# Output tiles summed in SBUF by VectorE, or copied by ScalarE and added to DRAM by transfers

## The chip, the cores and the metric

The kernel runs on one core of one Trainium2 chip. The core has five engines that run side by side, each with its own queue of instructions in a fixed order: TensorE (PE, matmuls), VectorE (DVE), ScalarE (ACT), GpSimd (POOL) and SyncE (SP, which here only issues transfers). They meet at semaphores: an instruction waits until another engine, or a transfer, has counted a semaphore up to a value. Transfers between DRAM (HBM) and on-chip memory (SBUF) can be issued from SP, ACT and POOL; sixteen transfer engines carry them out. PE writes its results to PSUM, which transfers and POOL don't read, so ACT or DVE must take them out.

The metric is the time on the device from start to end, in microseconds (us).

## The reference

For 2048 positions of 576 numbers, two branches over the same normalised input are added to the input:

```
xn  = layernorm(x)                                   # eps 1e-5, no weights
A   = attention(xn @ wqkv) @ wo                      # 32 heads of 18; each position sees
                                                     # itself and 7 earlier ones, 2 apart
B   = relu(xn @ w1) @ w2                             # 576 -> 4608 -> 576
out = x + A + B                                      # fp32
```

## The kernel before

Rows of x are taken so that row 16p + 2i + phase lies in partition p of tile i of a phase. There are two phases (even and odd rows), each with 8 tiles (i = 0..7) of 128 rows; because attention steps by 2, a phase never needs the other's rows. A tile is 128 partitions x 576 columns, 288 KB.

To come near fp32 accuracy, PE's operands are split into a high and a low part (`two`, `transpose_split`, `h_out`: ACT makes the high part, DVE subtracts to get the low part, for some early weights POOL does), and every product is a sum of matmuls of these parts.

The backbone is the feed-forward branch. Its hidden dimension is cut into 36 blocks of 128 columns; three blocks make a chunk, so a phase has 12 chunks. For each chunk the kernel walks over four pairs of tiles (tb = 0..3), and for each pair over the chunk's three blocks (f = 0..2). That gives 2 x 12 x 4 x 3 = 288 slots, in one list. In slot n:

- `run_splits` splits weights that are due and issues further weight loads on SP, through five staging buffers `st`;
- `h_mm` for slot n + 2: fourteen matmuls into a PSUM tile `ph` (two of these), then ACT's relu `hhi` (line 563) and DVE's `hlo` (line 566);
- whatever the plan has put into this slot (`todo`);
- `o_mm` for slot n: twelve matmuls from `hhi`, `hlo` and w2 into two PSUM tiles `po`, one for each tile of the pair. They collect over the three blocks; after the third, `o_out` adds them into the tiles of x in SBUF (line 620, DVE);
- what the plan has put behind (`todo_late`);
- `run_bg`: pieces of attention on DVE, in a queue `bg`. A piece is put in when the planner's own sum of DVE's costs (`t["dve"]`, raised by `dve(n)`) is no more than a margin ahead of its sum for PE (`t["pe"]`). So what is taken from DVE's sum moves attention pieces to earlier slots.

x tiles live in a pool `xp` of 11 buffers. A tile is loaded (`load_x`, line 245 on SP, or ACT for tile 1), gets its mean and variance (`stats`, lines 257 to 264, the reciprocal root on POOL), is normalised into `xn` (`norm`, line 276/277 on ACT or 279 on DVE), is transposed on PE (`make_xt`, lines 293/294) and split into `xT`. After that it stays as the accumulator of its output rows. In the other phase's preparation four tiles are transposed by DVE and DRAM instead of PE.

Four attention units per phase (8 heads each) have 8 steps of `qkv_tile` (q, k, v of one tile through PSUM tiles `pm`, copied out by ACT), then a queue of DVE pieces. One piece, the mask (line 434), is on POOL; the maximum on DVE (line 440) follows it. When the units are done, the wo product of each tile follows: `wo_a` transposes by 32 x 32 blocks on DVE and stores them to DRAM (`turned`), `wo_f` loads them back, `wo_s` splits, and `wo_b` multiplies by wo into two `pm` tiles, which DVE adds into the tile of x in two column ranges (`CUT`: 256 and 320; line 529). `done` counts for each tile the two last additions, the wo one and that of the last chunk; at the second SP stores the tile (line 537).

The head, before slot 4, is written out by hand: loads, statistics, transposes and the first three blocks in an order that follows the arrival of the data. `HEAD` lists what of it is left for slots 4 to 6, among it the statistics, normalisation and transposes of tiles 6 and 7. The end is by hand too: in the last slot each tile's additions and stores are in two column ranges (lines 626, 628).

Of the kernel before, what the change touches and what calls it, by code (L numbers as in the profile page):

```python
# [10 lines left out]
F32 = mybir.dt.float32  # L11
# [6 lines left out]
P = 128  # L18
NPH = 2
# [20 lines left out]
FIRST = 4  # L40

HEAD = (
    (4, 0, 'stats', 6, False, True),
    (4, 1, 'norm', 6, True),
    (4, 1, 'stats', 7),
# [10 lines left out]
def tile_body(ctx: ExitStack, tc: tile.TileContext, x, wqkv, wo, w1, w2, out):  # L56
# [15 lines left out]
    ctx.enter_context(tc.manual_schedule())  # L72
    pool = lambda name, bufs, **k: ctx.enter_context(tc.tile_pool(name=name, bufs=bufs, **k))
    consts = pool("consts", 1)
    xp = pool("xp", 11)
    xtp = pool("xtp", NTB)
    qop = pool("qop", 1)
    kp = pool("kp", 1)
# [33 lines left out]
    def mm(o, l, r, start, stop, n):  # L112
        nc.tensor.matmul(o, l, r, start=start, stop=stop)  # L113
        t["pe"] += n / 2400.0 + 0.002

    def dve(n):
        t["dve"] += (n + 130) / 960.0
# [403 lines left out]
    def wo_b(ph, i):  # L521
        d, w = OT.pop((ph, i)), WO[ph]
        po = [ps_m.tile([P, c.stop - c.start], F32, name="pm") for c in CUT]
        for j, (a, b) in enumerate(TERMS):
            for h, c in enumerate(CUT):
                mm(po[h], d[a], w[b][:, c], j == 0, j == len(TERMS) - 1, D2)
        for h, c in enumerate(CUT):
            acc = X[ph, i][:, c]
            nc.vector.tensor_tensor(acc, po[h], acc, op=ALU.add)  # L529
            dve(D2)  # L530

    left = {(ph, i): 2 for ph in range(NPH) for i in range(NI)}

    def done(ph, i):
        left[ph, i] -= 1
        if left[ph, i] == 0:
            nc.sync.dma_start(o_v[ph, i], X[ph, i])


    slots = [(ph, c, tb, f) for ph in range(NPH) for c in range(NCH) for tb in range(NTB) for f in range(C)]  # L540
# [38 lines left out]
    def half(po, h):  # L579
        if isinstance(po, list):  # L580
            return po[h]
        return po[:, 1, 0 : D - 256] if h else po[:, 0, 256:512]
# [28 lines left out]
    def o_out(n, which=range(2)):  # L611
        ph, c, tb, f = slots[n]
        if f < C - 1:
            return
        for k in which:
            i = 2 * tb + k
            acc = X[ph, i]
            if n < len(slots) - 1:
                whole = PO[k].rearrange("p b c -> p (b c)")[:, 256 : 256 + D]
                nc.vector.tensor_tensor(acc, whole, acc, op=ALU.add)  # L620
                dve(D)
                if c == NCH - 1:
                    done(ph, i)
                continue
            for h, c in reversed(list(enumerate(CUT))):
                nc.vector.tensor_tensor(acc[:, c], half(PO[k], h), acc[:, c], op=ALU.add)  # L626
                if k:
                    (nc.scalar if h else nc.sync).dma_start(o_v[ph, i][:, c], acc[:, c])
            if k == 0:
                done(ph, i)  # L630


    todo = {}
# [1 line left out]
    def at(n, f, *a):  # L635
        todo.setdefault(n, []).append((f, a))
# [7 lines left out]
    for ph in range(NPH):  # L644
        b = ph * SPP
        for c in range(NCH):
            for f in range(C):
                s = b + c * SPC + f
                first = ph == c == 0
                plan.append((HEADW[f] if first else s - 5, w1_task, ((ph, c, f), c * C + f)))  # L650
                plan.append((HEADW[3 + f] if first else s - 3, w2_task, ((ph, c, f), c * C + f)))
        for u in range(NU):
            s = b + UNIT0 + u * UNIT_STEP
            plan.append((s - 5, wq_tasks, ((ph, u), u)))
            for i in range(NI):
                at(s + i, qkv_tile, ph, u, i)
            late(s + NI + 1, attention, ph, u)
        s = b + UNIT0 + NU * UNIT_STEP + WO_AT
        plan.append((s - 8, wo_tasks, (ph,)))
        for i in range(NI):  # L660
            z = s + WO_STEPS[i]
            late(z, wo_a, ph, i)
            at(z + 1, wo_f, ph, i)
            late(z + 3, wo_s, ph, i)
            at(z + 4, wo_b, ph, i)
            at(z + 4, done, ph, i)
        if ph + 1 < NPH:
            e = b + SPP - SPC
            for i in range(NI):
                if i >= len(XT_STEPS):  # L670
                    z = e + 3 + 2 * i
                    at(z - 6, load_x, ph + 1, i)
                    late(z - 2, stats, ph + 1, i)
                    late(z - 1, norm, ph + 1, i)
                    at(z + 1, make_xt, ph + 1, i)
                    continue
                load, first, second, send, back, parts = (e + k for k in XT_STEPS[i])
                at(load, load_x, ph + 1, i)
                late(first, stats, ph + 1, i, False, True)
                late(second, norm_turned, ph + 1, i)  # L680
                late(send, xt_a, ph + 1, i)
                at(back, xt_f, ph + 1, i)
                at(parts, xt_s, ph + 1, i)
# [27 lines left out]
    h_terms(0, both)  # L711
    run_splits(-8)
    stage_more(4)
    for i in range(4, NI):
        load_x(0, i)
    stats(0, 2)
    for z in x0[2:], x1[2:]:
        for f in z:
# [46 lines left out]
    make_xt(0, 5, bank=ps_h)  # L765
    o_mm(3, which=(1,))
    for z, k, op, *a in HEAD:
        (late if k else at)(z, {"stats": stats, "norm": norm, "xt": make_xt}[op], 0, *a)
    M = (3.0, 1.5, 3.0)
    AT_WO = range(UNIT0 + NU * UNIT_STEP + WO_AT, UNIT0 + NU * UNIT_STEP + WO_AT + 12)  # L770
    for n in range(FIRST, len(slots)):
# [42 lines left out]
```

## Time and profile before

| | |
|---|---|
| median of 3 runs | 1167.42 us (1166.56 to 1168.52) |
| span of the profiled execution, first to last instruction | 1163.8 us |
| PE busy | 1155.9 us |
| DVE busy | 822.9 us |
| ACT busy | 308.1 us |
| POOL busy | 44.9 us |
| moved by transfers | 88.66 MB, a mean of 76 GB/s |

For the profiled execution the profile gives the span; the runs' times hold what lies around it as well.

How the profile's rows are read: L12 is line 12 of the kernel. A group's row has line, engine, operation, output<-inputs, their shapes and how many there are, then busy time in us and the mean of one in ns, then the idle time of the engine just before them with what ended most of it. A row of waits says which engine and line waited for which, with the total in us, the number of times and the longest. A row of a timeline begins with start and duration in us; x4 means that four instructions are merged. A row of windows has the stretch, its length, each engine's busy time and (x instructions), the granted clock of PE, the busy share of the transfer engines and GB/s. PEld is PE's loading of weights, which runs beside its matmuls; SPq and ACTq are transfers being issued. The chain is the work that ended last, followed back from the last instruction.

### The profile page before, as it was taken

What the parts mean: (1) busy time and instruction counts of PE and PEld (TensorE: products, weight loads), DVE (VectorE), ACT (ScalarE), POOL (GpSimd) and SP (SyncE); (2) the same over time, 40 slices, a digit from 0 to 9 for tenths busy, and PEclk for the clock granted to TensorE, in tenths of its full rate; (3) what the DMA queues carried; (4) which work ended last, traced back from release to release, by engine and by line L of the source; (5) the groups of instructions that cost most, each with busy time, mean ns of one, the idle gap of its engine ahead of it and who ended that gap; (6) DMA issues with size and microseconds to landing.
All of it is one profiled execution on the core that took longest, in us unless ns stands there. A gap on an engine that the chain in (4) does not pass through costs nothing.

```text
span 1163.8 us, 21695 instructions
## 1 busy us (share of the span) xinstructions
PE 1155.9 (99%) x8916; PEld 1147.9 (99%) x8916; DVE 822.9 (71%) x1300; ACT 308.1 (26%) x747; POOL 44.9 (4%) x60
## 2 busy tenths in 40 slices
PE   8999999999999999999999999999999999999998
PEld 8999999999999999999999999999999999999998
DVE  7427885887687688876683288768858877887843
ACT  4422222131231212322433123222222312222210
POOL 2200100010000000000010001000100000000000
PEclk9999999999999999999999999999999999999999
DMA  6303221140321211365752113021312303113541
GB/s 184 98 23 85 65 55 53 40 112 1 94 76 34 82 32 52 96 151 116 175 170 66 46 53 94 22 77 36 92 34 62 110 1 101 44 32 97 123 100 63
DMA packets 149732, 88.66 MB, mean 76 GB/s; under 512 B 58512, under 2 KB 133264, under 8 KB 149632
## 3 DMA queue, kind: packets, MB, share of 16 engines
q1 hardware_dynamic: 146656, 78.54, 25.1%
q10 hardware_dynamic: 2976, 8.72, 2.6%
q8 instruction: 70, 1.15, 0.4%
q14 instruction: 30, 0.25, 0.1%
HBM read 67.90 MB, written 11.14 MB: 68 GB/s over the span
## 4 chain that ended last, share of the span: by engine, by line
PE 99%; issue 0%; DVE 0%; DMA 0%; POOL 0%; ACT 0%; SPq 0%; DVEq 0%; POOLq 0%
PE ph L113 39%; PE po L113 38%; PE pm L113 20%; PE pm L293 0%; DMA x<-in_x 0%; DVE x L626 0%; POOL rstd L264 0%; PE pm L294 0%; PE po L293 0%; ACT xT L298 0%; DVE xn L279 0%; DVE bst L257 0%; SPq L243 0%; DVEq L810 0%; PE ph L294 0%
## 5 line engine op out<-in xcount | busy, mean ns | idle before, releaser
L113 PE MATMUL ph<-xT,w1t 128*128 128x256 f32 x4018 | 505.0, 277 | 0.7 <-ACT xT L298 0.7
L113 PEld LDWEIGHTS ph<-xT,w1t 128*128 128x128 f32 x4018 | 486.8, 188 | 1.3 <-ACT xT L298 1.0
L113 PE MATMUL po<-w2t,hhi 128*128 128x256 f32 x2292 | 393.0, 293 | 0.0
L113 PEld LDWEIGHTS po<-w2t,hhi 128*128 128x128 f32 x2292 | 335.4, 188 | 1.1
L563 ACT ACTIVATE hhi<-ph 128x256 fp32r<-128x256 f32 x287 | 110.0, 384 | 582.2 <-PE ph L113 568.9
L113 PE MATMUL po<-w2t,hlo 128*128 128x256 f32 x1146 | 242.4, 292 | 0.0
L566 DVE SCALAR_TENSOR_TENSOR hlo<-ph,hhi 128x256 fp32r<-128x256 f32 x287 | 121.0, 422 | 164.5 <-ACT hhi L563 164.0
L113 PEld LDWEIGHTS po<-w2t,hlo 128*128 128x128 f32 x1146 | 188.9, 187 | 0.0
L620 DVE TENSOR_TENSOR x<-po,x 128x576 f32<-128x576 f32 x190 | 143.1, 757 | 60.1 <-PE po L113 57.2
L113 PE MATMUL pm<-wq,xT 128*128 128x432 f32 x896 | 185.5, 358 | 0.0
L113 PEld LDWEIGHTS pm<-wq,xT 128*128 128x128 f32 x896 | 163.8, 188 | 5.6
L428 DVE TENSOR_TENSOR pr<-qo,k 128x1152 f32<-128x1152 f32 x64 | 86.1, 1349 | 0.0
L431 DVE TENSOR_REDUCE lg<-pr 128x64 f32<-128x1152 f32 x64 | 85.1, 1343 | 0.0
L458 DVE TENSOR_TENSOR pr<-lg,v 128x1152 f32<-128x1152 f32 x64 | 84.7, 1350 | 0.0
L152 DVE TENSOR_TENSOR w2t<-st,w2t 128x576 fp32r<-128x576 f32 x72 | 55.8, 775 | 32.4 <-ACT w2t L148 32.3
L152 DVE TENSOR_TENSOR w1t<-st,w1t 128x640 fp32r<-128x640 f32 x70 | 58.9, 841 | 20.6 <-ACT w1t L148 20.5
L465 DVE TENSOR_TENSOR pr<-pr 128x288 f32<-128x288 f32 (+1 forms) x128 | 70.6, 601 | 0.0
L148 ACT ACTIVATE w2t<-st 128x576 fp32r<-128x576 f32 x72 | 49.3, 684 | 44.9 <-PE po L113 32.5
L397 ACT ACTIVATE k<-pm 128x144 f32<-128x144 f32 x64 | 18.7, 292 | 146.3 <-PE pm L113 146.3
L148 ACT ACTIVATE w1t<-st 128x640 fp32r<-128x640 f32 x71 | 52.1, 734 | 11.7 <-DMA k<-k 6.0
L434 POOL TENSOR_SCALAR_AFFINE_SELECT lg<-lg 1x512 f32<-1x512 f32 x8 | 9.9, 1234 | 809.6 <-DVE lg L431 809.6
L529 DVE TENSOR_TENSOR x<-pm,x 128x256 f32<-128x256 f32 (+1 forms) x32 | 13.1, 453 | 30.2 <-PE pm L113 30.2
(85 smaller groups left out, 470.0 us busy)
## 6 DMA issues: line engine op xcount, KB each, us to landing
st<-in_w SPq DMA_DIRECT2D x72, 288.0 KB, 3.1
st<-in_w SPq DMA_DIRECT2D x72, 256.0 KB, 3.2
st<-in_wqkv SPq DMA_DIRECT2D x32, 216.0 KB, 3.0
turned<-tr SPq DMA_DIRECT2D x64, 80.0 KB, 3.0
xn<-turned SPq DMA_DIRECT2D x16, 320.0 KB, 3.2
st<-in_w SPq DMA_DIRECT2D x142, 32.0 KB, 2.9
out<-x SPq DMA_DIRECT2D x15, 288.0 KB, 2.1
x<-in_x SPq DMA_DIRECT2D x14, 288.0 KB, 4.3
```

What stands on the lines that cost most here:

```text
L113: nc.tensor.matmul(o, l, r, start=start, stop=stop)
L148: nc.scalar.activation(hi, src, AF.Copy)
L152: nc.vector.tensor_tensor(lo, src, f32(hi), op=ALU.subtract)
L397: nc.scalar.activation(k[:, W - 1 + i, :], pq[:, 1, :], AF.Copy)
L428: nc.vector.tensor_tensor(pr[i], q, window(k, i), op=ALU.mult)
L431: nc.vector.tensor_reduce(lg[:, i], pr.pop(i).rearrange(heads, d=Dh), axis=AX.X, op=ALU.add)
L458: nc.vector.tensor_tensor(pr[i].rearrange(heads, d=Dh), e, window(v, i).rearrange(heads, d=Dh), op=ALU.mult)
L465: nc.vector.tensor_tensor(o, z[:, 0:n], z[:, n : 2 * n], op=ALU.add)
L529: nc.vector.tensor_tensor(acc, po[h], acc, op=ALU.add)
L563: nc.scalar.activation(hi, pt, AF.Relu)
L566: nc.vector.scalar_tensor_tensor(lo, pt, 0.0, f32(hi), op0=ALU.max, op1=ALU.subtract)
L620: nc.vector.tensor_tensor(acc, whole, acc, op=ALU.add)
```

## The change

The output in DRAM becomes the accumulator. Early in the head SP issues one transfer that copies all of x into the output, 4.72 MB. From then on each finished tile, of `o_out` (190 whole ones, and two in halves at the end) and of `wo_b` (16), is copied from PSUM by ACT into one of four new buffers `ev`, and POOL issues a transfer that adds the buffer to the tile's rows of the output. x tiles aren't accumulators any more, so they are free after normalisation: `xp` shrinks from 11 to 6 buffers, and tiles 6 and 7 of the first phase are loaded in slot 4 in place of the head. `done` and its stores go. DVE's part of the planner's costs no longer has the additions.

In the built program PE's instructions are the same, in the same order. SP's copy stands where the load of tile 6 stood. POOL has 210 adding transfers in its queue. The first two stand between the reciprocal roots of tiles 4 and 5 and the subtractions for the first attention weights (wq); the first waits for the copy. Each transfer waits for ACT's copy and the transfer eight before it, some also for an earlier one of the same tile; a copy on ACT waits for the transfer four before it.

```diff
 HEAD = (
+    (4, 0, 'load', 6),
+    (4, 0, 'load', 7),
     (4, 0, 'stats', 6, False, True),
...
-    xp = pool("xp", 11)
+    xp = pool("xp", 6)
+    evp = pool("evp", 4)
...
         for j, (a, b) in enumerate(TERMS):
             for h, c in enumerate(CUT):
                 mm(po[h], d[a], w[b][:, c], j == 0, j == len(TERMS) - 1, D2)
+        ev = evp.tile([P, D], F32, name="ev")
         for h, c in enumerate(CUT):
-            acc = X[ph, i][:, c]
-            nc.vector.tensor_tensor(acc, po[h], acc, op=ALU.add)
-            dve(D2)
-
-    left = {(ph, i): 2 for ph in range(NPH) for i in range(NI)}
-
-    def done(ph, i):
-        left[ph, i] -= 1
-        if left[ph, i] == 0:
-            nc.sync.dma_start(o_v[ph, i], X[ph, i])
+            nc.scalar.activation(ev[:, c], po[h], AF.Copy)
+        add_out(ph, i, ev)
+
+    def add_out(ph, i, ev):
+        nc.gpsimd.dma_start(o_v[ph, i], ev, accum_op=ALU.add)
...
         for k in which:
             i = 2 * tb + k
-            acc = X[ph, i]
+            ev = evp.tile([P, D], F32, name="ev")
             if n < len(slots) - 1:
                 whole = PO[k].rearrange("p b c -> p (b c)")[:, 256 : 256 + D]
-                nc.vector.tensor_tensor(acc, whole, acc, op=ALU.add)
-                dve(D)
-                if c == NCH - 1:
-                    done(ph, i)
+                nc.scalar.activation(ev, whole, AF.Copy)
+                add_out(ph, i, ev)
                 continue
             for h, c in reversed(list(enumerate(CUT))):
-                nc.vector.tensor_tensor(acc[:, c], half(PO[k], h), acc[:, c], op=ALU.add)
-                if k:
-                    (nc.scalar if h else nc.sync).dma_start(o_v[ph, i][:, c], acc[:, c])
-            if k == 0:
-                done(ph, i)
+                nc.scalar.activation(ev[:, c], half(PO[k], h), AF.Copy)
+                nc.gpsimd.dma_start(o_v[ph, i][:, c], ev[:, c], accum_op=ALU.add)
...
-            at(z + 4, done, ph, i)
...
     stage_more(4)
-    for i in range(4, NI):
+    for i in range(4, 6):
         load_x(0, i)
+    nc.sync.dma_start(out.rearrange("(p r) d -> p (r d)", p=P), x.rearrange("(p r) d -> p (r d)", p=P))
     stats(0, 2)
...
     for z, k, op, *a in HEAD:
-        (late if k else at)(z, {"stats": stats, "norm": norm, "xt": make_xt}[op], 0, *a)
+        (late if k else at)(z, {"load": load_x, "stats": stats, "norm": norm, "xt": make_xt}[op], 0, *a)
```

## The prediction

> **What bounds the kernel now.** I read the page first: busy times, slices, the chain, the groups.
>
> ```profile
> span 1163.8 us, 21695 instructions
> PE 1155.9 (99%) x8916; PEld 1147.9 (99%) x8916; DVE 822.9 (71%) x1300; ACT 308.1 (26%) x747; POOL 44.9 (4%) x60
> PE 99%; issue 0%; DVE 0%; DMA 0%; POOL 0%; ACT 0%; SPq 0%; DVEq 0%; POOLq 0%
> L563 ACT ACTIVATE hhi<-ph 128x256 fp32r<-128x256 f32 x287 | 110.0, 384 | 582.2 <-PE ph L113 568.9
> L620 DVE TENSOR_TENSOR x<-po,x 128x576 f32<-128x576 f32 x190 | 143.1, 757 | 60.1 <-PE po L113 57.2
> L113 PE MATMUL ph<-xT,w1t 128*128 128x256 f32 x4018 | 505.0, 277 | 0.7 <-ACT xT L298 0.7
> ```
>
> PE is the chain: 1155.9 of 1163.8 us. ACT spends 569 us waiting for PE, and the 190 adds of L620 wait for PE too (57.2 us). Next I asked what PE itself waited for, over the whole span.
>
> ```profile
> PE po L293 <- DVE xn L279: 1.8, 1, 1.8
> PE po L104 <- POOL mhalf L99: 1.4, 1, 1.4
> PE ph L113 <- ACT xT L298: 0.7, 1, 0.7
> PE pm L293 <- ACT xn L277: 0.3, 1, 0.3
> ```
>
> Four waits, 4.2 us together, once each, before the first transposes and the first ph; PE never waits for an add. So the 143 us of adds in L620, and the 32 smaller ones of the wo steps, that the change takes off DVE buy nothing: PE's matmuls are the same in number and order, and its idle time is 7.9 us in all. What the change can do is put a wait into PE's queue, at the head, in the loop or at the end.
>
> **The head: a transfer ahead of two loads.** In a timeline of the first 40 us, SP's queue and the work on tile 6 of x:
>
> ```profile
> 11.22 1.85 SPq L245 DMA_DIRECT2D x<-in_x  x4
> 13.17 4.70 SPq L198 DMA_DIRECT2D st<-in_wqkv  x4
> 28.83 1.46 ACT L148 ACTIVATE wq<-st 128x432 fp32r<-128x432 f32 x3
> 29.46 3.30 POOL L150 TENSOR_TENSOR wq<-st,wq 128x432 fp32r<-128x432 f32 x3 [4.13 <-ACT wq L148]
> 30.61 0.38 SPq L160 DMA_DIRECT2D st<-in_w  x1
> 31.80 0.81 DVE L257 BATCH_NORM_STATS2 bst<-x 128x6 f32<-128x288 f32 x2
> 32.88 0.59 SPq L170 DMA_DIRECT2D st<-in_w  x1
> 34.07 0.78 ACT L277 ACTIVATE xn<-xn,rstd 128x576 f32<-128x576 f32 x1
> 35.60 0.60 PE L293 MATMUL pm<-ident,xn 128*128 128x128 f32 x4
> DMA to landing us min/median/max: 2.2/4.4/5.9
> ```
>
> The four x loads at 11.22 are tiles 4 to 7. Tile 6 goes through statistics (31.80) and two ACT passes, ready at 34.85; PE reaches its transposes at 35.60. From statistics to ready: 3.05 us; spare on PE: 0.75 us.
>
> In the changed program tiles 6 and 7 are loaded in step 4, on SP behind the three w1 pieces (30.61 to 33.47). The first piece waits for a staging buffer that POOL's first wq subtraction frees (29.46 plus a third of 3.30). So even with nothing else late, tile 6 is issued at 33.47, lands 3.0 later (between 2.2 and 4.4) and is ready at 39.5: PE waits **3.9 us** (3.1 to 5.3).
>
> More is added. The copy of x into the output, 4.72 MB, takes the place of tile 6 on SP, at about 12.15. POOL's first adding transfer waits for it, and POOL's wq subtractions stand behind two such transfers; SP's second w1 piece waits for the copy as well. When does the copy end? By windows of 2.5 us (last columns: clock, DMA share, GB/s):
>
> ```profile
> 10.00:12.50 2.50, 2.21 (x16) 2.01 (x17) 2.12 (x7) 1.90 (x5) 2.37 (x3) 1.00 1.00 312
> 12.50:15.00 2.50, 2.50 (x24) 2.50 (x23) 2.41 (x5) 1.61 (x4) 0.52 (x2) 1.00 1.02 334
> 15.00:17.50 2.50, 2.50 (x23) 2.50 (x22) 2.43 (x8) 1.90 (x5) 0.80 (x1) 1.00 1.00 343
> 17.50:20.00 2.50, 2.50 (x21) 2.50 (x21) 2.28 (x5) 0.16 (x1) 0.22 (x1) 1.00 0.80 243
> 20.00:22.50 2.50, 2.50 (x22) 2.50 (x21) 1.93 (x5) 0.59 (x2) 0.00 (x0) 1.00 0.39 98
> ```
>
> The transfer engines are full from 10 to 17.5. From 12.1 on they move 2.68 MB (0.13, 0.83, 0.86, 0.61, 0.25), of which 1.69 MB are issued after 12.1 (two x tiles of 0.295, four wq pieces of 0.221, two of 0.11). So 0.99 MB stand ahead of the copy: 3.0 us at 334 GB/s. The copy itself isn't in the trace. At the loads' 343 GB/s it takes 13.8 us. If a byte that is read from DRAM and written there counts twice, 27.5 us. No row lies nearer to either, so I take the middle, 21 us. A landing of 2.1 us on top (the store row below) gives 12.15 + 3.0 + 21 + 2.1 = **38.2** (31.0 to 44.7).
>
> A rule to set beside this: the Trainium skill's page "DMA: Bandwidth & Descriptors", "Latency and other measured facts", has copies between HBM tensors at 207 to 214 GB/s. By it the copy takes 22.4 us and ends at 39.6, 1.4 us later than mine.
>
> Issue times, from the tile view of turned (ns, min/median/max), and two landings of the page:
>
> ```profile
> L334 SPq DMA_DIRECT2D turned<-tr x64: 302/511/2242, 497.7 to 1123.5; - x64
> out<-x SPq DMA_DIRECT2D x15, 288.0 KB, 2.1
> st<-in_w SPq DMA_DIRECT2D x72, 288.0 KB, 3.1
> ```
>
> A transfer issued by GpSimd isn't in the trace. Bounds for what it holds POOL: 0.38 us (the issue at 30.61) and 2.24 us (the longest of turned). I take 1.0, between them and nearer to the common ones. After the copy: two issues 2.0, the wq subtraction 1.1, the w1 pieces 1.5 (0.38, a median 0.51 for the second, 0.59), landing 3.0, tile 6's work 3.05: ready at 38.2 + 10.65 = 48.9, against 35.6. PE waits **13.3 us** in place of the 3.9, not on top (6.1 for an early copy, 19.8 for a late one; POOL's issues move it by -1.2 to +2.5). What stands behind tile 6 on DVE and ACT is released with it. Tile 7's statistics follow directly, and PE has fourteen ph matmuls between the two tiles' transposes, so tile 7 adds nothing. ACT's first new copies, of step 2, delay tiles 4 and 5 by some tenths, which fall into this wait.
>
> **The loop.** 206 transfers, and 190 whole copies on ACT plus 32 halves. From the forms on ACT and a timeline of the plain loop:
>
> ```profile
> L298 ACT ACTIVATE xT<-pm 128x512 fp32r<-128x512 f32 x11 | 6.6, 599 | 5.0 <-PE pm L293 4.7
> 95.99 1.54 DVE L620 TENSOR_TENSOR x<-po,x 128x576 f32<-128x576 f32 x2
> 96.57 1.76 PE L113 MATMUL ph<-xT,w1t 128*128 128x256 f32 x14
> 98.17 0.68 PE L113 MATMUL po<-w2t,hhi 128*128 128x256 f32 x4
> 105.45 1.54 DVE L620 TENSOR_TENSOR x<-po,x 128x576 f32<-128x576 f32 x2
> ```
>
> A 512-column copy took 599 ns and a 256-column one 384, so 576 take about 0.65: 190 x 0.65 + 16 x 0.82 = 137 us more on ACT, which has 850 free. Two copies end about 0.7 us after PE's second half; PE returns to that PSUM after 1.6 us of ph matmuls. Cover: 0.9 us. Cost nothing; without that cover it is the part of 1.3 us that sticks out, 95 times.
>
> Pairs come every 9.46 us, and an output buffer is used again after four copies: a transfer has some 17 us, against 3 for a load. The issues take 2 of POOL's 9.46 us. A third place is the mask: in all eight units it now stands on POOL right behind a pair, and the maximum on DVE waits for it.
>
> ```profile
> DVE m L440 <- POOL lg L434: 5.4, 4, 1.6
> L431 DVE TENSOR_REDUCE lg<-pr 128x64 f32<-128x1152 f32 x64 | 85.1, 1343 | 0.0
> L514 ACT ACTIVATE oT<-xn 128x640 fp32r<-128x640 f32 x16 | 11.8, 736 | 24.9 <-PE pm L113 24.3 <-DMA xn<-turned 0.6
> 500.00:520.00 20.00, 20.00 (x163) 20.00 (x162) 14.07 (x28) 5.37 (x10) 0.00 (x0) 1.00 0.74 166
> ```
>
> The last scores come some 3.7 us after the pair's matmuls (1.6 of ph, about 0.8 for hhi and hlo, L431's 1.34), the two issues are through after 2, so the mask is late only if an issue takes over 1.8. In the wo steps the transfer engines are at 0.74 already and ACT once waited 0.6 us for a turned tile; twice as many adding transfers as elsewhere make that tighter. For both I take 1 us (0 to 8, half a microsecond in each of sixteen wo steps).
>
> **The end.**
>
> ```profile
> 1159.01 0.82 DVE L626 TENSOR_TENSOR x<-po,x 128x320 f32<-128x320 f32 x2 [2.72 <-PE po L113]
> 1159.83 0.28 PE L113 MATMUL pm<-w2t,hlo 128*128 128x256 f32 x1
> 1160.65 0.33 SPq L628 DMA_DIRECT2D out<-x  x1
> ```
>
> PE ends at 1160.11; the last store is issued at 1160.65 and lands 2.1 later, 1162.75. The first half tile is ready for a copy at 1159.0. Now four transfers leave POOL one after the other from 1159.4: the last starts at 1162.4 and, as it also reads, takes 3.1: 1165.5, **+2.8** (0 with 0.38 per issue, +8.6 with 2.24 and, as the sum of a load and a store, a landing of 5.2).
>
> **Sum.** 1163.8 + 13.3 + 1 + 2.8 = 1180.9. The median of the runs is 3.6 above this execution's span; added, **1184.5 us**.
>
> **Rivals.** *The copy is done before anyone needs it* (by 28): only the late load is left, 3.9 + 2.8, time 1174. For it: the engines are free from 22.5. Against: 4.72 MB would have to pass in 11 us, at 430 GB/s, and no window shows over 343. But two waits of mine may be shorter. Chance 0.24.
> *Late copy and crowded wo steps together*: 19.8 + 8 + 4, time 1199. Chance 0.10.
> *The adding transfers are too slow*: the loop is theirs once one takes over 4.73 us of the queue (9.46 for two). At 6 us: 206 x 6 = 1236 plus the head, 1260. For it: each reads its destination as well. Against: a store's whole landing is 2.1. Chance 0.06. The skill's "Collectives: The Full Stack", section on why ReduceScatter is half of AllGather, says that an add in the transfer engines halves the rate, for its two reads. By it 0.295 MB at half of 343 GB/s take 1.7 us, and the loop stays PE's; no run so far shows it.
> *Not slower*: matmuls gain from fewer DVE reads of PSUM. To win back 17.1 us each of 8916 would have to shorten by 1.9 ns; from there the time is 1167 or less. Against: the fourteen ph matmuls beside two adds take 0.126 us each (1.76 / 14, at 96.57), which is the mean of all 4018 (505.0). Chance 0.05.
> That transfers to different tiles wait for one another, and so do not overlap, the built program excludes: each waits for its copy, a buffer and its own tile's last one.
>
> **How the numbers follow.** Forecast 0.55, rivals 0.24, 0.10, 0.06, 0.05. Range 1172 to 1200: from the late load alone with a cheap end (3.9 + 0.5) to the late copy with crowded steps; left out are the slow transfers, the rival of no loss and the edges, together 2 in 10. Likeliest one's own range: 1177 to 1194. About 0.2% (2.3 us) is what a measurement can tell from no change; the late load alone is 3.1 or more. Faster 0.02, same 0.04, slower 0.94.
>
> **What would show it.** One long PE wait near 36 to 49 us for tile 6's normalised x; the copy landing near 38; POOL's first adding transfer right after it; no PE wait between 60 and 1100 us; DVE near 670 us, ACT near 445; the end 2 to 3 us longer after the last matmul. Wrong if PE's wait in the head is under 3 us, if PE waits in the plain loop, or if the copy lands before 30.

## The result, and the profile after

| | median, us | lowest to highest | span of the profiled execution |
|---|---|---|---|
| before | 1166.99 | 1165.77 to 1168.52 | 1163.8 |
| after | 1231.56 | 1230.0 to 1236.77 | 1230.6 |

The ratio is 1.0559 (95% interval 1.0534 to 1.0585): the change makes the kernel 5.6% slower. The forecast was 1184.5, the range 1172 to 1200. The direction was right; the time lies 31.6 us above the range.

The rows of the changed kernel's page that answer to those of before, busy times first:

```profile
span 1230.6 us, 22188 instructions
PE 1171.2 (95%) x8916; PEld 1157.7 (94%) x8916; DVE 669.3 (54%) x1074; ACT 433.4 (35%) x973; POOL 223.3 (18%) x270
DMA packets 177640, 150.04 MB, mean 122 GB/s; under 512 B 61616, under 2 KB 136624, under 8 KB 177440
q0 software_dynamic: 30240, 61.36, 35.8%
L536 POOL DMA_DIRECT2D out<-ev x206 | 181.4, 937 | 932.2 <-ACT ev L619 816.7
L619 ACT ACTIVATE ev<-po 128x576 f32<-128x576 f32 x190 | 122.3, 652 | 45.4 <-PE po L116 20.8
```

PE has the same 8916 matmuls, but 95% of the span instead of 99%: its idle time grew from 7.9 to 59.4 us, and its busy time by 15.3 us. ACT's copies took 652 ns (0.65 forecast) and POOL's issues 0.94 us (1.0). q0 is the queue of GpSimd's transfers, in packets, MB and share of the 16 transfer engines: 35.8% of 1230.6 us for 208 tiles' worth (61.36 MB / 0.295) is 2.12 us of all sixteen engines for one tile, counted by the time that the packets took.

Next, what PE waited for, over the whole span (total, times, longest). Before, all of PE's waits came to 4.2 us.

```profile
PE pm L116 <- ACT oT L517: 16.2, 7, 6.3
PE ph L116 <- DVE hlo L565: 15.9, 11, 4.5
PE pm L296 <- ACT xn L280: 7.0, 1, 7.0
PE po L116 <- ACT ev L619: 5.2, 4, 1.6
```

Only the third row, tile 6 in the head, was forecast with a size of its own. The first belongs to the wo steps (oT is the turned tile that `wo_s` splits); the second to the loop, where the lower half of the hidden block (`hlo`) comes late (its longest, 4.5 us, to the change of phase, where the next phase's x is loaded, normalised and transposed); the fourth to ACT's copies out of PSUM.

Where along the span the time goes can be read from PE's own order, which is the same in both programs: the start of its n-th matmul after, less that of the same matmul before, from the two traces.

| n-th matmul of PE (start before, us) | late by, us | grew by |
|---|---|---|
| 750 (106.0), head done | 11.0 | 11.0 |
| 4000 (526.1), plain loop of the first phase | 21.3 | 10.3 |
| 4750 (619.6), wo steps and change of phase | 43.0 | 21.7 |
| 8250 (1076.8), plain loop of the second phase | 53.9 | 10.9 |
| 8916 (1159.8), wo steps of the second phase | 59.1 | 5.2 |
| end of the span | 66.8 | 7.7 |

The largest single part, 21.7 us, stands in a stretch for which the forecast had 1 us, together with the mask. In a timeline of that stretch, first of the kernel before, then of the changed one (SP's queue and those who wait for it):

```profile
541.65 2.04 SPq L334 DMA_DIRECT2D turned<-tr  x4
547.14 0.38 SPq L507 DMA_DIRECT2D xn<-turned  x1
```

```profile
564.02 8.61 SPq L337 DMA_DIRECT2D turned<-tr  x4
572.72 0.45 SPq L184 DMA_DIRECT2D st<-in_w  x1
573.02 0.74 ACT L517 ACTIVATE oT<-xn 128x640 fp32r<-128x640 f32 x1 [8.20 <-DMA xn<-turned]
573.81 1.54 PE L116 MATMUL pm<-wq,oT 128*128 128x256 f32 x5 [6.26 <-ACT oT L517]
```

Before, SP issued the four stores of a turned tile in 2.04 us. Here, in the longest case, they hold SP for 8.61 us; the w2 load stands behind them in the queue, the turned tile loaded ahead of them lands late, ACT waits 8.20 us for it and PE 6.26 for ACT.

### The profile page after: what moved, and what is told of

The parts are those of the page before. It is cut to its first block, busy times and chain, and to the rows that moved or that the text cites. A ratio compares the mean times of both kernels' runs of the same rounds, so it can differ in the third digit from the quotient of the medians.

```text
span 1230.6 us, 22188 instructions
## 1 busy us (share of the span) xinstructions
PE 1171.2 (95%) x8916; PEld 1157.7 (94%) x8916; DVE 669.3 (54%) x1074; ACT 433.4 (35%) x973; POOL 223.3 (18%) x270
## 3 DMA queue, kind: packets, MB, share of 16 engines
q0 software_dynamic: 30240, 61.36, 35.8%
## 5 line engine op out<-in xcount | busy, mean ns | idle before, releaser
L116 PE MATMUL ph<-xT,w1t 128*128 128x256 f32 x4018 | 509.5, 278 | 16.6 <-DVE hlo L565 15.9
L536 POOL DMA_DIRECT2D out<-ev x206 | 181.4, 937 | 932.2 <-ACT ev L619 816.7
L619 ACT ACTIVATE ev<-po 128x576 f32<-128x576 f32 x190 | 122.3, 652 | 45.4 <-PE po L116 20.8
L155 DVE TENSOR_TENSOR w2t<-st,w2t 128x576 fp32r<-128x576 f32 x72 | 54.1, 751 | 77.6 <-ACT w2t L151 77.4
L116 PE MATMUL pm<-wq,oT 128*128 128x256 f32 x224 | 37.8, 311 | 16.2 <-ACT oT L517 16.2
```

The source lines that it names most:

```text
L155: nc.vector.tensor_tensor(lo, src, f32(hi), op=ALU.subtract)
L536: nc.gpsimd.dma_start(o_v[ph, i], ev, accum_op=ALU.add)
L619: nc.scalar.activation(ev, whole, AF.Copy)
```

## The experiments

Two theories stood at the start. **P**, the planner: without VectorE's additions in its sum it moves attention pieces to earlier slots, where they meet the splits of weights on ACT and DVE, and `hlo` comes late. **A**, the adding: a transfer that adds holds the transfer engines longer than one that writes, and what SP issues beside it (turned tiles, weights) comes late (the expectations of e1 and e3 call this one T). Beside them the head, ACT's place and the end are tested one by one. Each kernel was timed against the kernel before (1166.6 to 1168.2 us in these runs).

**e1: the planner's sum kept.**

```diff
             nc.scalar.activation(ev[:, c], po[h], AF.Copy)
+            dve(D2)
...
                 nc.scalar.activation(ev, whole, AF.Copy)
+                dve(D)
```

> The changed kernel, with the additions' cost kept in the planner's sum for DVE (dve(D) and dve(D2) stay), so that the attention pieces stand about where they stood before the change; computes the same. Theory P (the loop's waits of PE for hlo come from attention pieces that moved earlier and now meet the weight splits): the 15.9 us of waits for hlo go almost all away, time 1231.6 - 16 = about 1214, and the wo steps' 16.2 us for oT stay. Theory T (the adding transfers make the loads land later, wherever the pieces stand): waits for hlo stay above 10 us, time 1226 or more.

**e2: write, don't add.**

```diff
-        nc.gpsimd.dma_start(o_v[ph, i], ev, accum_op=ALU.add)
+        nc.gpsimd.dma_start(o_v[ph, i], ev)
...
-                nc.gpsimd.dma_start(o_v[ph, i][:, c], ev[:, c], accum_op=ALU.add)
+                nc.gpsimd.dma_start(o_v[ph, i][:, c], ev[:, c])
```

> The changed kernel, with transfers that write the tile instead of adding it; leaves out the sum over chunks (the output holds each tile's last piece). If the cost is in the adding (each transfer reads its destination too): a transfer lands in about 3 us instead of 5.7, the turned stores in about 3.5 instead of 5.0, and the waits of PE for hlo, oT and ev together fall from 37 to under 15 us; with the clock that comes with it about 1200. If any 210 transfers of 288 KB do it: 1225 or more, landings as in the changed kernel.

**e3: few adding transfers.**

```diff
                 nc.scalar.activation(ev, whole, AF.Copy)
-                add_out(ph, i, ev)
+                if c == NCH - 1:
+                    add_out(ph, i, ev)
```

> The changed kernel, with ACT's copies all kept, but adding transfers only for the last chunk and the wo tiles (leaves out the other 176 pieces of the sum). Theory T: the loop's waits for hlo fall under 3 us; what is left is the head (11), the wo steps (up to 25, as their transfers stay), ACT's place behind its own k and v transfers (5) and the end (8): 1200 to 1215. Theory P: waits for hlo stay above 10 us, 1222 or more.

**e4: tiles 6 and 7 loaded in the head, ahead of the copy.**

```diff
-    (4, 0, 'load', 6),
-    (4, 0, 'load', 7),
...
-    for i in range(4, 6):
+    for i in range(4, NI):
         load_x(0, i)
```

> The changed kernel, with tiles 6 and 7 loaded in the head again, ahead of the copy of x (their buffers are those of tiles 0 and 1, free by then); computes the same. Theory of the prediction's head (the late load of tile 6 behind the copy is PE's 7.0 us wait, and the half clock of 3.4 us follows from it): PE's wait for xn before 45 us goes to under 1 us, the half clock at 40 us goes too, time down by 8 to 11: about 1221. Rival (the wq splits behind the copy hold ACT as long): a wait of 4 us or more stays, 1227 or more.

| | time, us | ratio (95%) | late at matmul 750 / 4000 / 4750 / 8250 / last / end |
|---|---|---|---|
| after | 1231.56 | 1.0559 (1.0534 to 1.0585) | 11.0 / 21.3 / 43.0 / 53.9 / 59.1 / 66.8 |
| e1 | 1214.05 | 1.0417 (1.0379 to 1.0456) | 11.9 / 16.6 / 31.0 / 34.6 / 40.0 / 47.8 |
| e2 | 1197.17 | 1.0280 (1.0230 to 1.0330) | 11.1 / 16.9 / 16.8 / 24.0 / 24.0 / 31.5 |
| e3 | 1197.35 | 1.0262 (1.0242 to 1.0282) | 10.0 / 13.7 / 23.6 / 28.3 / 28.3 / 33.1 |
| e4 | 1226.12 | 1.0529 (1.0457 to 1.0602) | 5.6 / 19.3 / 36.3 / 48.8 / 52.9 / 60.5 |

Both theories hold a part. e1's time is the one that P gives. In the waits of e1 the row of `hlo` is gone altogether and that of oT stays:

```profile
PE pm L116 <- ACT oT L517: 15.2, 8, 4.0
PE po L116 <- ACT ev L620: 7.3, 7, 1.6
PE pm L296 <- ACT xn L280: 7.2, 1, 7.2
```

In e2 it is the other way round, the oT row is gone and `hlo` has 5.6 us left:

```profile
PE ph L116 <- DVE hlo L565: 5.6, 8, 1.5
PE pm L296 <- ACT xn L280: 5.5, 1, 5.5
PE po L116 <- ACT ev L619: 5.0, 4, 1.5
```

The queue's row on e2's page gives the price of the adding itself:

```profile
q0 software_dynamic: 16672, 61.36, 13.6%
```

The same 61.36 MB as after, in little more than half the packets, and 0.78 us of all sixteen engines for a tile (13.6% of 1195.3 over 208) instead of 2.12. An adding transfer costs the engines 2.7 times a writing one. The rule that the prediction set beside its rival on slow transfers, the Trainium skill's "Collectives: The Full Stack", "Why ReduceScatter is half of AllGather", has half the rate; the direction agrees, the traces give a factor of 2.7 here.

e3 fits neither theory as it was written. Its time, 1197.35, lies just under the range of the one (1200 to 1215) and far from the other's 1222; PE's waits for `hlo` are 8.0 us, neither under 3 nor over 10. And its wait for oT is 1.0 us, although all sixteen wo tiles still add: with twelve adding transfers in the wo steps of a phase in place of twenty, the turned tiles are hardly late.

e4 takes 5.4 us off the late head, by the medians and by the traces at matmul 750; 8 to 11 were expected. The wait for tile 6 falls from 7.0 to 2.3 us, not under 1. Its three runs lie between 1223.95 and 1236.65, so the median alone would not carry this size.

**e5: planner's sum kept, and writing.** Both edits of e1 and e2.

> The changed kernel with both earlier edits at once: the planner is still told of the adds that VectorE no longer does (as in e1), and the transfers write and don't add (as in e2; this leaves out the residual sum). Theory 'two causes that share nothing': the gains of e1 (17.5 us) and e2 (34.4 us) add up, 1231.6 - 51.9 = about 1180 us. Rival 'the two overlap in the wo steps, and what is left is the rest': the late head (9 us), PE's waits for the copies behind ScalarE's halo transfers (5 to 7 us) and the longer end (7.5 us) stay, 1167 + 22 to 24 = about 1189 to 1191 us. In both, no PE wait for oT and hlo.

**e6: VectorE copies.**

```diff
-                nc.scalar.activation(ev, whole, AF.Copy)
+                nc.vector.tensor_copy(ev, whole)
+                dve(D)
```

and so in `wo_b` and at the end.

> The changed kernel with the planner's sum kept as in e1, and the copy PSUM to ev done by VectorE where VectorE added before; the adding transfers stay. Theory A (what is left beyond the planner's shift is the adding transfers and the late head): as e1, 1214 us, less the 5 to 7 us of PE's waits for ev behind ScalarE's halo transfers, so 1207 to 1209 us, and PE's wait for oT stays near 15 us. Rival 'ScalarE is too crowded in the wo steps': the oT waits fall below 5 us with the copies gone from ScalarE, and the time is below 1200 us.

**e7: the halo transfers on SP.** These are a unit's four transfers that copy the edge rows of k and v to the next partition; ACT issues them.

```diff
-                    nc.scalar.dma_start(z[a + 1 : b + 1, 0 : W - 1, :], z[a:b, NI : NI + W - 1, :])
+                    nc.sync.dma_start(z[a + 1 : b + 1, 0 : W - 1, :], z[a:b, NI : NI + W - 1, :])
```

> The changed kernel with the four halo transfers per unit of k and v issued by SP and not by ScalarE. Theory: the copies wait in ScalarE's order behind these transfers (3.3 us, four times), PE's wait for ev (5.2 us, four times) goes away and the time falls by 5 to 6 us, to about 1226 us. Rival: SP's queue is as full, attention starts later and DVE's plan slips, or the 5 us are given back at the next wait for oT: 1229 to 1233 us.

**e8: the end issued as before.**

```diff
-                nc.gpsimd.dma_start(o_v[ph, i][:, c], ev[:, c], accum_op=ALU.add)
+                (nc.scalar if h else nc.sync).dma_start(o_v[ph, i][:, c], ev[:, c])
```

> The changed kernel, but the last four half tiles are written by SP and ScalarE without adding, as the kernel before issued them (this leaves out the residual sum of the last two tiles). Theory: the 7.7 us by which the end is longer than before are GpSimd's issue of four transfers one after the other (3.5 us), their longer way to DRAM and GpSimd's drain, and at least 5 us go: 1224 to 1226.5 us, with 4 to 6 us from the last matmul's start to the span's end (11.7 now). Rival: the end waits for the queue's earlier adding transfers anyway: 1230 to 1232 us.

| | time, us | ratio (95%) | late at matmul 750 / 4000 / 4750 / 8250 / last / end |
|---|---|---|---|
| e5 | 1188.57 | 1.0191 (1.0169 to 1.0212) | 10.8 / 12.2 / 15.5 / 18.7 / 18.7 / 26.2 |
| e6 | 1210.88 | 1.0364 (1.0332 to 1.0396) | 10.4 / 17.4 / 31.9 / 33.9 / 37.5 / 45.4 |
| e7 | 1228.67 | 1.0532 (1.0514 to 1.0550) | 9.4 / 22.2 / 39.5 / 50.0 / 54.7 / 62.7 |
| e8 | 1222.94 | 1.0484 (1.0467 to 1.0500) | 10.8 / 20.8 / 36.5 / 49.4 / 54.1 / 55.9 |

e5 is the rival of its expectation: the two causes overlap (51.9 us apart, 43.0 together). What is left is 21.9 us over before by the medians; of the 26.2 in its profile 10.8 are the head, 7.5 the end and 7.9 the loop and the wo steps; no wait for `hlo` is left, and one of 3.0 us for oT.

e6 fits A only loosely: the wo steps still lose 14.5 us with no copy on ACT, while PE's wait for oT falls to 7.5 us, between the theory's 15 and the rival's 5, and the time, 1210.9, is 2 us above the theory's and far from the rival's 1200. So ACT's copies aren't what the wo steps suffer from.

e7 took the `ev` wait from 5.2 to 1.3 us, but only 2.9 us off the time, between the 5 to 6 of the theory and the rival; part of the gain is given back elsewhere, and where wasn't followed up.

e8, 8.6 us faster where 5 to 7.6 were expected, shows the end. In a timeline, GpSimd's four transfers after, and the last of ACT's and SP's in e8:

```profile
1218.90 3.54 POOL L624 DMA_DIRECT2D out<-ev  x4 [3.96 <-ACT ev L623]
1218.94 0.28 PE L116 MATMUL pm<-w2t,hlo 128*128 128x256 f32 x1
```

```profile
1213.89 0.28 PE L116 MATMUL pm<-w2t,hlo 128*128 128x256 f32 x1
1215.53 0.35 SPq L624 DMA_DIRECT2D out<-ev  x1
```

From the start of the last matmul to the end of the span it is 11.7 us after (1230.6 - 1218.94) and 5.8 in e8 (1219.7 - 1213.89). e2's end is 11.4 us with GpSimd's transfers writing (1195.3 less its last matmul at 1183.9), so at the end it isn't the adding but the issuer that costs. GpSimd's four issues end 3.5 us after the last matmul starts (1222.44) and 8.2 us before the span does; SP's last issue ends at 2.0, and 3.8 before.

**e9: three repairs together**: e1's planner sum, e4's loads, e7's halo transfers. **With lead**: also the wo steps' split and matmuls one step later.

```diff
-            late(z + 3, wo_s, ph, i)
-            at(z + 4, wo_b, ph, i)
+            late(z + 4, wo_s, ph, i)
+            at(z + 5, wo_b, ph, i)
```

> The whole change, sum and all, with three repairs at once: the planner's sum kept (e1, 1214.1), tiles 6 and 7 loaded ahead of the copy (e4, 5.4 us less) and the halo transfers issued by SP (e7, 2.9 us less). Theory 'the repairs add up, the adding transfers in the wo steps stay': 1214.1 - 5.4 - 2.9 = about 1206 us, with PE's waits for oT near 15 us and none over 2 us outside the wo steps. Rival 'each only moves a wait to the next': 1210 to 1214 us.

> As the kernel with the three repairs, and in the wo steps the split of a tile and its matmuls come one step later (steps 4 and 5 after its transpose and not 3 and 4), so the transfers to DRAM and back have a step, 7 to 8 us, more. Theory 'the adding transfers only make these transfers late': PE's waits for oT fall below 4 us and the time lies 8 to 16 us under that of the three repairs alone. Rival 'it isn't lateness of these tiles, the loads of weights behind them are as late': at most 4 us less.

**e10: writing in the wo steps alone.**

```diff
-        nc.gpsimd.dma_start(o_v[ph, i], ev, accum_op=ALU.add)
+        if calm:
+            nc.gpsimd.dma_start(o_v[ph, i], ev)
+        else:
+            nc.gpsimd.dma_start(o_v[ph, i], ev, accum_op=ALU.add)
...
-        add_out(ph, i, ev)
+            dve(D2)
+        add_out(ph, i, ev, True)
...
-                add_out(ph, i, ev)
+                dve(D)
+                add_out(ph, i, ev, 120 <= n % SPP < 138)
```

> The changed kernel with the planner's sum kept (e1, 1214.1), where the transfers from steps 120 to 137 of each phase, which are the 16 wo tiles and the 12 pieces a phase that end in those steps, write and don't add (their part of the residual sum is left out); the other 146 pieces add. Theory 'adding costs only where the wo steps' own transfers run': nearly all of the 25.5 us that e5 gains over e1 goes, 1189 to 1192 us. Rival 'adding costs everywhere, by the load on the engines': by the share of transfers, about a fifth to a quarter goes, 1207 to 1209 us.

| | time, us | ratio (95%) | late at matmul 750 / 4000 / 4750 / 8250 / last / end |
|---|---|---|---|
| e9 | 1205.30 | 1.0321 (1.0287 to 1.0354) | 6.1 / 8.9 / 29.1 / 30.3 / 35.2 / 43.1 |
| e9 with lead | 1202.43 | 1.0295 (1.0273 to 1.0317) | 5.6 / 7.7 / 28.2 / 29.4 / 34.5 / 42.1 |
| e10 | 1190.66 | 1.0200 (1.0185 to 1.0215) | 12.2 / 14.5 / 14.5 / 17.5 / 17.5 / 25.1 |

e10 is the run that settles the place: 40 of the transfers write, 166 whole ones still add (not 146, as the expectation counts), and the loss between matmuls 4000 and 4750 is 0.0 us instead of e1's 14.4. It is within 2.1 us of e5, where none adds; the intervals of the two overlap. So, with the planner's sum kept, adding costs some 2 us or nothing in 166 places, and 23.4 us (1214.05 - 1190.66) in the 40 of the wo steps. Without it the plain loops feel the adding too: they lose 21.2 us after and 13.0 in e2, where nothing adds.

e9's time fits "the repairs add up", but single runs of it lie between 1200.24 and 1208.66, and two waits over 2 us stand outside the wo steps that weren't expected (3.7 for tile 6, 4.1 for `hlo` at the change of phase); its plain loops are nearly free of loss (2.8 us up to matmul 4000 and 1.2 in the second phase), and 20.2 of its 43.1 us are the first wo steps.

One more step for the turned tiles doesn't help, within the intervals; that is the rival of its expectation. ACT no longer waits for turned tiles there (16.9 us in e9), but it waits 34.4 us for the w2 loads that stand behind them in SP's queue (27.5 in e9) and once 12.8 us for SP's stores of the next phase's x (`words`; 6.3 in e9). The split of oT stands behind both in ACT's order, and PE still waits 17.6 us for it. So it isn't a delay that a little slack covers; what SP issues next is late as well.

**e11 and e12: the disputed load by itself.** The kernel before, its own work unchanged, with additional transfers of x tiles to a DRAM tile that nothing reads, in the same 40 places as in e10; adding in e11, writing in e12.

```diff
+    apart = pool("apart", 1, space=bass.MemoryType.DRAM).tile([P, NI, D], F32, name="apart")
...
             nc.vector.tensor_tensor(acc, po[h], acc, op=ALU.add)
             dve(D2)
+        more(ph, i)
+
+    def more(ph, i):
+        nc.gpsimd.dma_start(apart[:, i], X[ph, i], accum_op=ALU.add)
...
                 dve(D)
+                if 120 <= n % SPP < 138:
+                    more(ph, i)
```

> The kernel before, with 40 additional transfers of 288 KB that GpSimd issues in steps 120 to 137 of the two phases, after VectorE's adds there; each adds a tile of x to a DRAM tile of its own, which nothing reads (8 plain transfers fill it early). ScalarE has no copies, the planner is told nothing new, SP issues what it issued. Theory 'the adding transfers' load on the DMA engines holds up the turned tiles and the weights by itself': e1 less e10 cost 23 us for the same 40, so 15 to 25 us more than before, 1182 to 1192 us, and PE waits for oT or hlo there. Rival 'it needs ScalarE's copies or the planner's shift': under 4 us more, 1167 to 1171 us.

> The kernel before with the same 40 additional transfers, which write and don't add. Theory 'the load of adding': plain transfers cost little, 0 to 4 us, 1167 to 1171 us. Rival 'any additional transfer there costs, adding or not': more than half of what the adding ones cost.

**e13: all repairs, and VectorE at the end.** The kernel with lead, where the partial sums of the last two tiles are loaded back and the last additions are VectorE's.

```diff
+    def load_sum(ph, i):
+        X[ph, i] = xp.tile([P, D], F32, name="x")
+        nc.sync.dma_start(X[ph, i], o_v[ph, i])
...
-                nc.scalar.activation(ev[:, c], half(PO[k], h), AF.Copy)
-                nc.gpsimd.dma_start(o_v[ph, i][:, c], ev[:, c], accum_op=ALU.add)
+                nc.vector.tensor_tensor(ev[:, c], half(PO[k], h), X[ph, i][:, c], op=ALU.add)
+                (nc.scalar if h else nc.sync).dma_start(o_v[ph, i][:, c], ev[:, c])
...
+    for i in (NI - 2, NI - 1):
+        at(len(slots) - 4, load_sum, NPH - 1, i)
```

> The whole change, sum and all, with the three repairs and the later split, and at the end the partial sums of the last two tiles loaded back four steps earlier, added by VectorE and stored by SP and ScalarE as the kernel before did. Theory: the 5.8 us that e8 gained at the end are gained here too, 1202.4 - 5.8 = 1196 to 1198 us. Rival: the load of the partial sum comes late behind the adding transfers and the end stays as long: 1201 to 1204 us.

| | time, us | ratio (95%) | late at matmul 750 / 4000 / 4750 / 8250 / last / end |
|---|---|---|---|
| e11 | 1190.49 | 1.0199 (1.0169 to 1.0228) | 0.0 / 2.9 / 22.6 / 22.6 / 25.9 / 26.2 |
| e12 | 1171.19 | 1.0039 (1.0024 to 1.0054) | 2.7 / 2.6 / 5.8 / 5.8 / 6.6 / 6.8 |
| e13 | 1196.69 | 1.0260 (1.0238 to 1.0283) | 5.3 / 7.1 / 21.3 / 23.0 / 27.9 / 29.7 |

Forty adding transfers beside the untouched kernel cost 23.4 us, as much as e1 less e10; the same forty writing cost 4.1 (of the 6.8 us in its profile, 2.7 are lost in the first 40 us, before the first of them). Neither ACT's copies nor the planner is needed. In e11's waits, PE's and ACT's, stand oT and the turned tiles again; the last row is the changed kernel's own:

```profile
PE pm L114 <- ACT oT L515: 9.4, 4, 4.1
PE pm L114 <- ACT hhi L571: 3.9, 1, 3.9
ACT oT L515 <- DMA xn<-turned: 34.7, 8, 7.0
```

```profile
ACT oT L517 <- DMA xn<-turned: 23.7, 11, 8.2
```

Before, ACT waited 0.6 us for turned tiles; in e10 it is 0.6 again, in e12 5.6.

And this is where the transfers are held up: SP's issues of the turned tiles, min/median/max in ns, in the tile view of `turned`; after, e11, e12 and e10 in this order (before: 302/511/2242).

```profile
L337 SPq DMA_DIRECT2D turned<-tr x64: 303/698/2949, 517.1 to 1186.5; - x64
```

```profile
L335 SPq DMA_DIRECT2D turned<-tr x64: 302/722/4908, 497.6 to 1151.3; - x64
```

```profile
L335 SPq DMA_DIRECT2D turned<-tr x64: 302/526/1642, 500.3 to 1130.1; - x64
```

```profile
L337 SPq DMA_DIRECT2D turned<-tr x64: 302/522/1687, 511.8 to 1141.4; - x64
```

With adding transfers in the wo steps the median rises from 0.51 to 0.7 us (0.69 in e1); without them it is as before. The longest rises to 2.9 and 4.9, but is 2.3 in e1, so the median is the better sign. SP issues in order, so whatever stands behind a store that takes long to issue is late with it.

e13 gains the 5.7 us of the end and is the best of the change with its sum intact; it is 2.6% slower than before, and more than half of what it loses is still in the wo steps.

## Why the prediction was right in direction and wrong in size

**The premise held.** PE is the chain, its matmuls and their order are the same, and DVE's additions bought nothing: DVE is at 669.3 us (about 670 foretold), ACT at 433.4 (445); before, PE had never waited for an addition.

**The head: the mechanism right, the copy mis-sized.** In the timeline and the row of transfers of the changed kernel's first 60 us:

```profile
out<-in_x SPq DMA_DIRECT2D x1, 4608.0 KB, 18.0
```

```profile
30.59 1.97 POOL L536 DMA_DIRECT2D out<-ev  x2 [5.44 <-DMA out<-in_x]
35.57 1.06 SPq L248 DMA_DIRECT2D x<-in_x  x2
39.45 0.82 DVE L260 BATCH_NORM_STATS2 bst<-x 128x6 f32<-128x288 f32 x2 [5.49 <-DMA x<-in_x]
42.57 1.12 PE L296 MATMUL pm<-ident,xn 128*128 128x128 f32 x4 [7.05 <-ACT xn L280]
```

The copy was issued at 12.0 and landed at 30.0, 18.0 us later with the queue ahead of it; the forecast had 38.2 (31.0 to 44.7), from a copy of 21 us in the middle of 13.8 and 27.5. Less the 3.0 us of queue and the 2.1 of landing that the forecast put beside it, 12.9 us are left for the copy: the lower end, 13.8, was the near one, and the byte isn't counted twice. Even all 18.0 us give 262 GB/s. The prediction quoted 207 to 214 from the Trainium skill's "DMA: Bandwidth & Descriptors", "Latency and other measured facts", where they are measured on tiles of 16 KiB rows inside wider tensors; for this copy of one contiguous tensor the trace doesn't agree with them. POOL's first transfers follow the landing, and their two issues took 1.97 us against 2.0. With the landing put right, the prediction's own chain gives 30.0 + 10.65 - 35.6 = 5 us; PE waited 7.0, for tile 6, as one wait. Of the 2 us between, 0.9 are tile 6's landing (35.57 to 39.45 in place of 3.0 us), the rest the w1 pieces ahead of it. The condition "wrong if the copy lands before 30" sits on its edge. The wait isn't the whole loss: at matmul 750 PE is 11.0 late, as the clock fell to half behind it (below). 13.3 was forecast for the head, so this term didn't make the time too low.

**The loop's cover.** A cover of 0.9 us over the copies and a price of nothing stood there. It holds for 186 of the 190 copies. In the other four the copy stands in ACT's order behind the halo transfers of k and v, which ACT itself issues, and ACT waits 3 us there for one of them to land:

```profile
ACT ev L619 <- DMA k<-k: 12.3, 4, 3.3
```

That is the 5.2 us of PE's `ev` wait (1.3 in e7, where SP issues them); what is queued ahead on the engine that takes over a step had not been asked.

**The failed step: the two places at "1 us (0 to 8)", beside a loop at nothing.** From the head's end to the last matmul the forecast had 1 us; in the traces it is 48.1 (59.1 - 11.0), 26.9 in the two stretches with the wo steps and 21.2 in the plain loops. Two things were left out of it: what adding transfers do to SP's transfers in the wo steps, and what the planner does when DVE's costs go.

**The wo steps.** The prediction priced an adding transfer by its time on the clock, some 17 us until its buffer is needed against 3 for a load, and the wo steps by "half a microsecond in each of sixteen". It didn't add up the time that the transfers take of the sixteen engines in that stretch. The queues' rows for the stretch from matmul 4000 to 4750, first before, then after:

```profile
q1 hardware_dynamic: 33536, 13.47, 55.2%
```

```profile
q1 hardware_dynamic: 36303, 12.91, 45.4%
q0 software_dynamic: 3135, 6.41, 38.4%
out<-ev POOLq DMA_DIRECT2D x20, 288.0 KB, 6.5
```

Before, 55.2% of 94 us are 52 us of engine time. After, 45.4 and 38.4% of a stretch that has grown to 116 us are 97 us, more than the 94 in which PE's work there was done before. From rows of before the sum could have been made, as an estimate: 0.295 MB at 343 GB/s, twice as it also reads, is 1.7 us; 20 of them and 52 make 86 of 94. The same rows of e10 (94 us) and of e11 (113 us):

```profile
q1 hardware_dynamic: 33847, 12.27, 51.2%
q0 software_dynamic: 2115, 5.91, 28.0%
```

```profile
q1 hardware_dynamic: 35801, 15.06, 52.2%
q0 software_dynamic: 1870, 3.82, 22.7%
```

e10's are 74 us of engine time, and it loses nothing there; e11's are 85, and it loses 19.7 us. They differ in place as well: twelve of e10's twenty transfers in the stretch write, and its eight additions are issued from 595.4 us on, after its last store of a turned tile (564.6); e11's twelve additions are issued from 535.9 us on, its last turned tile is stored at 562.0. Whether the amount or the place within the stretch decides, these two don't separate. Shown is that the same forty transfers cost 23 us as additions and 4 as writes, and that what comes late are SP's stores and loads in the same engines, which PE waits for a few steps later. That they are the same engines, whoever issues, the Trainium skill says in "DMA: Bandwidth & Descriptors", "Issuing engines are not separate DMA queues"; the issue times of SP above agree.

The second phase's wo steps cost only 5.2 us after and 3.3 in e11. There x isn't loaded, turned and brought back for a next phase, as in the first. That this difference is the reason wasn't tested by a run of its own.

**The planner**, the other half of that term, was seen only at the mask. Two rows of waits after, and the second of them before:

```profile
DVE m L443 <- POOL lg L437: 13.4, 8, 2.1
ACT lg L447 <- DVE lg L446: 35.5, 8, 5.0
```

```profile
ACT lg L444 <- DVE lg L443: 17.2, 4, 5.3
```

The mask was 5.4 us in four waits before. A single wait is hardly longer than it was (2.1 against 1.6 us at most, 5.0 against 5.3 for the exponential's input); there are twice as many, one in each of the eight units. What the prediction feared did happen in four of them: POOL waits for the scores in only four (7.5 us), in the others it comes to the mask late, straight from its issues. But with the planner's sum kept (e1) POOL waits for the scores in all eight (19.6 us), and the two rows are 5.1 us in four and 9.9 in two, though POOL issues the same transfers. So it is the earlier slots of the pieces that bring the waits, not the issues by themselves. While ACT waits up to 5.0 us for the exponential's input, the splits of the weights, `hhi` and with it `hlo` stand behind it in ACT's order. That PE's 15.9 us for `hlo` go with the planner's sum is shown by e1; that they come about in this way is read from the order. e1 loses 8.3 us in the plain loops, where the changed kernel loses 21.2. Keeping the planner's sum is worth 17.5 us (1231.56 - 1214.05) with adding and 8.6 (1197.17 - 1188.57) without it.

**The end: right mechanism, too small.** 7.7 us in place of 2.8, inside its bounds (0 to 8.6). The four issues were sized at 1.0 each and took 0.89. What was too small is what follows them: from the last issue to the end it is 8.2 us after and 2.8 before (1163.8 less 1160.98), 5.4 more, where 1.0 had been put. How much of it is landing and how much GpSimd's own finish isn't separated.

**The rivals.** None came out. The transfers "too slow" would have had one over 4.73 us of the engines; it is 2.12, and the plain loop stays PE's. The rival was about the mean over the loop, and the greater loss was in one stretch. "Late copy and crowded wo steps" named the right place, with 8 us for it and the mask; the two stretches lost 21.7 + 5.2. Of the signs, "no PE wait between 60 and 1100 us" failed, and that PE waits in the plain loop is what was set down as showing the prediction wrong.

How the 64.6 us come together, from the medians: adding in the wo steps, with the change of phase, 23.4 (e1 less e10; e11 less before), the planner 8.6 to 17.5, end 5.7 to 8.6 (e13, e8), head 5.4 of its 11 (e4), halo transfers 2.9 (e7). The parts overlap, so they aren't a sum; e5 leaves 21.9 over before without adding and planner shift.

## What to carry to other kernels

Price a transfer in the time that it takes of the shared engines, not in its latency, and add that up for the busiest stretch: with the planner's sum kept, adding cost some 2 us in 166 places and 23 us in 40 others. Work taken off an engine that isn't the bound can still cost, if a planner fills the gap, and work given to an idle engine waits behind whatever that engine has queued. When a load is suspected, put it alone beside the old kernel (e11): one run says whether it needs the rest of the change.

## What the runs showed of the hardware beyond that

PE's clock fell to half behind waits. In windows of the changed kernel (third column from the end: granted clock):

```profile
36.00:40.00 4.00, 0.00 (x0) 0.00 (x0) 0.55 (x2) 0.00 (x0) 0.00 (x0) 1.00 1.01 298
40.00:47.00 7.00, 4.43 (x21) 4.40 (x22) 3.70 (x11) 4.57 (x10) 5.01 (x8) 0.51 0.39 103
47.00:60.00 13.00, 13.00 (x92) 12.79 (x91) 3.90 (x7) 4.34 (x13) 1.74 (x3) 1.00 0.49 121
573.00:580.00 7.00, 6.19 (x28) 6.19 (x29) 3.28 (x9) 1.01 (x2) 0.77 (x2) 0.54 0.69 150
```

In the clock records of all the runs every wait of PE of 3.2 us or more brought a stretch at half clock, of 3.41, 6.83 or 10.24 us; of waits between 1.4 and 3.0 us some did (2.16 in e9, 2.91 after), others didn't (2.96 in e4, 2.99 in e5). So the 7.0 us wait of the changed kernel, with 6.83 us at half clock behind it, cost up to 3.4 more. The Trainium skill's "TensorE: Matmul & The Clock Gate", "What's actually happening", has windows of 3.4 us that run freely and an idle one halving the clock; the lengths agree. Of the 15.3 us by which PE's busy time grew this is up to 10: the four stretches in the body of the changed kernel are 20.5 us long, and half of that is lost at most. Where the rest comes from wasn't looked into.

An adding transfer of 288 KB was cut into 144 packets where the writing one has 80 (30240 for 210 transfers of after, 3840 for the 48 of e12), and its landing took 5.7 us in the median against 2.7 (after, then e2):

```profile
out<-ev POOLq DMA_DIRECT2D x206, 288.0 KB, 5.7
```

```profile
out<-ev POOLq DMA_DIRECT2D x206, 288.0 KB, 2.7
```
